# Forty-four drains at the head of TensorE's instructions in a fused scan and two-MLP kernel, and a constant of the same name

## The chip, the cores and the metric

One core of one Trainium2 chip runs the whole program. The metric is the device time of one execution in microseconds (us); lower is better. Engines are named as in the profile: PE is TensorE's products, PEld its weight loads, DVE is VectorE, ACT ScalarE, POOL GpSimd, SP SyncE; a name with a q (PEldq) is an engine's sequencer, which carries out drains and waits on semaphores.

## The reference

Three stages follow each other: a gated linear recurrence over 768 steps for 4 batches of 8 heads of width 48, an MLP with x·cos(x) between its products, and an MLP with a maximum over three products.

```python
for t in range(768):
    state = alpha[:, :, t, :, None] * state + einsum('bhd,bhe->bhde', k[:, :, t], v[:, :, t])
    y[:, :, t] = einsum('bhd,bhde->bhe', q[:, :, t], state)
x = y.transpose(0, 2, 1, 3).reshape(3072, 384)
h = x @ w_in                      # 384 -> 2048
x = (h * cos(h)) @ w_out          # 2048 -> 384
h = maximum(maximum(x @ w1, x @ w2), x @ w3)   # 384 -> 768
out = h @ w_out2                  # 768 -> 384
```

## The kernel before, in words

Tokens are worked on in six units of 512. The recurrence is turned into products on chunks of 64 steps: a **visit** (`visit`, lines 658 to 769) makes the scores, the state's increments and the outputs for one pair of heads, in small products of 48 or 64 rows that run on quarters of the array (lines 679, 683, 697 and 704). A visit that serves a new pair and an old one has 128 products in the trace, and each product has a weight load of its own, so it is 256 instructions. The first unit is done ahead in another form (lines 500 to 600).

The first MLP (`moe1`) takes 16 steps per unit, 96 in all. A step has nine products into a bank of PSUM (lines 780 to 782) and nine that add to three accumulators (lines 811 to 813), all of 128 rows and 512 columns; each number is split into a high and a low part in fp32r, so that three products stand for one. Visits are strewn between these steps until about 370 us. The second MLP works in 18 cells by a scheme with fewer products (lines 1164 to 1166), and `down` closes each third (lines 1073 to 1075). All of these are 128x512 products too.

What stands where is set by a planner in the program (`Program.order`): each operation has a duration, a due time and a number of instructions, and the planner lays them out in time on every engine, with PSUM banks. It counts TensorE's instructions in blocks of 256 (`BLOCK`, line 287) and tells by it where a large visit may stand; the warm-up operation counts as 28 instructions there. Where several PSUM banks are free, which of two tiles gets which bank follows from the order of a set of names, so that two builds of one text can differ in bank numbers, and in the number of waiting instructions on TensorE (80 to 85).

TensorE's first operation is `warm` (lines 1271 to 1274): seven products of the identity matrix with itself into banks that nothing reads. It waits for the identity, which POOL writes (masks.py, lines 197 and 199). After it come two products that clear accumulators (line 525), then the first transposes (line 562) and scores (line 502) of the first unit.

SBUF is allotted from two ends. From the left come the constants and the recurrence's tiles; at the right end stand the first MLP's weights `wih`, `wil`, `woh`, `wol`, the tiles `gg` with x·cos(x), `yy0`, and, last, a filler tile:

```python
PAD = 88                                                   # line 65
wp.tile([P, PAD], F32, name="pad")                         # line 335
np_.tile([P, PAD], F32, name="pad2")                       # line 842
```

The second MLP's tiles `bs_1`, `fs`, `wf` and `x` take the same right end later, with a filler of the same width behind them.

Of the kernel before, what the change touches and what calls it, by code (L numbers as in the profile page):

```python
# [64 lines left out]
PAD = 88  # L65
# [17 lines left out]
LOD = (1, 3)  # L83

W1E = 21
MOE_EARLY = 5
EARLY = 3
FIRST = -4
# [16 lines left out]
class Program:  # L105
# [16 lines left out]
    def op(self, eng, dur, fn, reads=(), writes=(), due=0.0, nbytes=None, port=False, tiled=False, count=6, tag=None):  # L122
        n = len(self.ops)
        if tag:
            self.tags[tag] = n
        deps = set()
        for k in reads:
            if k in self.last_write:
                deps.add(self.last_write[k])
        for k in writes:  # L130
            if k in self.last_write:
                deps.add(self.last_write[k])
            deps.update(self.readers.get(k, ()))
        for k in writes:
            self.last_write[k] = n
            self.readers[k] = []
        for k in reads:
            self.readers.setdefault(k, []).append(n)
        for k in {*reads, *writes}:
            if isinstance(k, tuple) and k[0] == "ps":  # L140
                self.of_bank.setdefault(k, []).append(n)
        deps.discard(n)
        port = port or (eng == "Pool" and nbytes is None)
        self.ops.append((eng, dur, nbytes, fn, sorted(deps), due, port, tiled, count))
        return n
# [116 lines left out]
def act(n, psum=False):  # L262
    return (0.05 if psum else 0.095) + 0.00084 * n
# [41 lines left out]
def tile_kernel(ctx, tc, aa, qk, vv, vr, wt, outT):  # L305
    nc = tc.nc
    ve, se, ge, pe = nc.vector, nc.scalar, nc.gpsimd, nc.tensor
# [464 lines left out]
    def moe1(i):  # L772
# [13 lines left out]
        qk = ("q", qn)  # L786
        m = i - MOE_EARLY
        op("Act", act(HB, True), lambda: se.activation(q.bitcast(I32), ps, AF.Copy, bias=0.25, scale=INV2PI), [hk], [qk], m)  # L788
# [438 lines left out]
    def build():  # L1227
# [41 lines left out]
        op("Pool", 1.0, setup_rest, (), ["tri"], due=-98)  # L1269

        def warm():
            for x, n in ((acc[0], P), (acc[1], D), *((x, D) for x in ps_b)):
                m = ident[:, 0:n].rearrange("p (a b) -> p a b", a=1).to_broadcast([P, 4, n])
                pe.matmul(x[:, 0:4 * n].rearrange("p (a b) -> p a b", a=4), ident, m, start=True, stop=True)

        op("PE", WARM, warm, ["ident"], [("acc", 0), ("acc", 1)], due=-99, count=28)

        events = []

        def at(t, f, *a):  # L1280
            events.append((t, len(events), f, a))
# [12 lines left out]
        for f in range(NF1):  # L1294
            at(W0 + f / 100, weight1, f, "i", f - W1E)
            at(W0 + f / 100, weight1, f, "o", f - W1E + 1)
        for i in range(NS):
# [159 lines left out]
```

## Time and profile before

| | |
|---|---|
| time, median of 3 runs | 738.92 us (738.33 to 741.87) |
| the profiled execution | 738.8 us, of which 737.0 us lie from its first instruction to its last |
| PE busy | 730.9 us (99%), 5813 products |
| PEld busy | 601.8 us (82%), 5813 loads |
| DVE busy | 541.2 us (73%) |
| ACT busy | 419.9 us (57%) |
| POOL busy | 305.3 us (41%) |
| DMA | 120.41 MB, mean 163 GB/s |

The profiled execution lies 0.1 us under the median of the runs; 1.8 us of it are outside the span. An end of a product is modelled in the profile, so a small wait can hide inside a busy time; starts are measured, and the distance between two starts is what can be read best. A reader looks first at the shares, then at TensorE's waits, then at the first 8 us in order of time.

### The profile page before, as it was taken

The page shows a single profiled execution, that of the slowest core. Times are in us where ns is not written, and L with a number is a line of the kernel's source. Part 1 is how long each engine was busy: PE and PEld are TensorE (multiplying, and loading weights), DVE is VectorE, ACT ScalarE, POOL GpSimd, SP SyncE. Part 2 cuts the span into 40 slices and gives each one's busy share as a digit, 9 for nine tenths or more (in the row PEclk, how much of TensorE's full clock was granted, in tenths as well). Part 3 has the DMA queues.
Part 4 walks back from the last instruction along what each step waited for, and adds up shares of the span by engine and source line. Part 5 has one row for each costly group of instructions (what it writes and reads, how often), then busy time and mean ns, then how long its engine had stood idle before and what let it go on. Part 6 is the DMA issues. An engine that isn't in the chain of part 4 may idle for free.

```text
span 737.0 us, 14864 instructions
## 1 busy us (share of the span) xinstructions
PE 730.9 (99%) x5813; PEld 601.8 (82%) x5813; DVE 541.2 (73%) x859; ACT 419.9 (57%) x801; POOL 305.3 (41%) x287
## 2 busy tenths in 40 slices
PE   9999999999999999999999999999999999999997
PEld 7787888888888888888888888888888888888886
DVE  8999996878887776865655666467787768677763
ACT  4878766666756666667644655443563345634233
POOL 6444433556533635454320211043465543614442
PEclk9999999999999999999999999999999999999999
DMA  9876544564644654554250111397636556246302
GB/s 320 297 225 219 165 126 134 178 221 160 196 146 154 189 179 139 182 178 150 96 207 0 44 43 44 135 370 291 215 104 197 202 176 204 79 149 204 132 1 85
DMA packets 47525, 120.41 MB, mean 163 GB/s; under 512 B 4736, under 2 KB 19968, under 8 KB 42464
## 3 DMA queue, kind: packets, MB, share of 16 engines
q1 hardware_dynamic: 47456, 119.48, 48.5%
q8 instruction: 45, 0.74, 0.4%
q14 instruction: 24, 0.20, 0.1%
HBM read 91.54 MB, written 25.95 MB: 159 GB/s over the span
## 4 chain that ended last, share of the span: by engine, by line
PE 92%; DVE 3%; DMA 2%; ACT 1%; issue 1%; POOL 0%; DVEq 0%; ACTq 0%; POOLq 0%
PE acc L811 9%; PE acc L813 8%; PE acc L812 8%; PE ps L780 8%; PE ps L781 8%; PE ps L782 8%; PE ps L1164 6%; PE ps L1166 5%; PE ps L1165 5%; PE acc L1164 3%; PE acc L1166 3%; PE acc L1165 3%; PE acc L1075 2%; PE acc L1073 2%; PE acc L1074 2%; DMA raw<-in_wt 2%
## 5 line engine op out<-in xcount | busy, mean ns | idle before, releaser
L780 PE MATMUL ps<-xt,wih 128*128 128x512 f32 x288 | 114.5, 398 | 0.0
L811 PE MATMUL acc<-gg,woh 128*128 128x512 f32 x288 | 114.4, 397 | 0.0
L813 PE MATMUL acc<-gg,woh 128*128 128x512 f32 x288 | 112.4, 390 | 0.0
L812 PE MATMUL acc<-gg,wol 128*128 128x512 f32 x288 | 112.2, 390 | 0.0
L782 PE MATMUL ps<-xt,wil 128*128 128x512 f32 x288 | 112.2, 390 | 0.0
L781 PE MATMUL ps<-xt,wih 128*128 128x512 f32 x288 | 112.1, 389 | 0.0
L789 DVE SCALAR_TENSOR_TENSOR q<-q,ps 128x512 f32<-128x512 int32 x96 | 65.5, 683 | 37.7 <-ACT q L788 37.2
L790 ACT ACTIVATE q<-q 128x512 f32<-128x512 f32 x96 | 60.4, 631 | 40.0 <-DVE q L789 39.7
L794 DVE TENSOR_TENSOR gg<-q,gg 128x512 fp32r<-128x512 f32 x81 | 63.5, 788 | 23.2 <-ACT gg L793 22.6
L792 DVE TENSOR_TENSOR q<-q,ps 128x512 f32<-128x512 f32 x81 | 55.2, 682 | 32.9 <-ACT q L790 32.3
L788 ACT ACTIVATE q<-ps 128x512 int32<-128x512 f32 x96 | 56.8, 593 | 38.8 <-PE ps L782 37.1
L793 ACT ACTIVATE gg<-q 128x512 fp32r<-128x512 f32 x81 | 51.1, 631 | 36.0 <-DVE q L792 31.6
L954 POOL TENSOR_TENSOR ar<-ar,ar 128x512 f32<-128x512 f32 x21 | 28.8, 1377 | 92.2 <-DVE as L963 67.6
L813 PEld LDWEIGHTS acc<-gg,woh 128*128 128x128 f32 x288 | 54.1, 188 | 12.2 <-DVE gg L806 0.4
L811 PEld LDWEIGHTS acc<-gg,woh 128*128 128x128 f32 x288 | 54.1, 188 | 11.6
L782 PEld LDWEIGHTS ps<-xt,wil 128*128 128x128 f32 x288 | 54.1, 188 | 11.4
L780 PEld LDWEIGHTS ps<-xt,wih 128*128 128x128 f32 x288 | 54.1, 188 | 11.3 <-issue 0.2
L812 PEld LDWEIGHTS acc<-gg,wol 128*128 128x128 f32 x288 | 54.1, 188 | 10.5
L781 PEld LDWEIGHTS ps<-xt,wih 128*128 128x128 f32 x288 | 54.1, 188 | 10.3
L1172 ACT ACTIVATE q<-acc 128x512 f32<-128x512 f32 x36 | 21.5, 597 | 69.2 <-PE acc L1166 68.5
L1183 POOL TENSOR_TENSOR xf<-q 128x512 f32<-128x512 f32 x18 | 24.5, 1361 | 81.5 <-ACT q L1172 81.5
L1036 ACT ACTIVATE fs<-x 128x512 fp32r<-128x512 f32 x42 | 26.2, 630 | 44.8 <-DVE x L1187 30.0
(190 smaller groups left out, 1730.2 us busy)
## 6 DMA issues: line engine op xcount, KB each, us to landing
bs<-bfd SPq DMA_DIRECT2D x36, 1024.0 KB, 5.0
raw<-in_wt SPq DMA_DIRECT2D x56, 384.0 KB, 4.1
bfd<-bs SPq DMA_DIRECT2D x32, 384.0 KB, 3.0
kq<-in_qk SPq DMA_DIRECT2D x20, 512.0 KB, 4.6
al<-in_aa SPq DMA_DIRECT2D x23, 261.0 KB, 3.3
x1r<-yy SPq DMA_DIRECT2D x18, 256.0 KB, 2.1
ar<-x1r SPq DMA_DIRECT2D x18, 256.0 KB, 3.1
v<-in_vv SPq DMA_DIRECT2D x23, 192.0 KB, 4.9
```

The costliest lines, as they stand in the source:

```text
L780: pe.matmul(ps, wi["h"][:, f, cc], xt[:, cc, 0], start=(cc == 0), stop=False)
L781: pe.matmul(ps, wi["h"][:, f, cc], xt[:, cc, 1], start=False, stop=False)
L782: pe.matmul(ps, wi["l"][:, f, cc], xt[:, cc, 0], start=False, stop=(cc == NR - 1))
L789: op("DVE", dve(HB), lambda: ve.scalar_tensor_tensor(q, q.bitcast(I32), -TWOPI, ps, ALU.mult, ALU.add), [hk], [qk], m, tag=("rest", i))
L790: op("Act", act(HB), lambda: se.activation(q, q, AF.Sin, bias=0.5 * math.pi), (), [qk], m, tag=("sine", i))
L794: op("DVE", dve(HB), lambda: ve.tensor_tensor(gl, q, gh.bitcast(F32), ALU.subtract), [qk, ("gh", gn)], [("gl", gn)], m, port=True)
L811: pe.matmul(acc[c], oh, gh, start=(f == 0), stop=False)
L812: pe.matmul(acc[c], ol, gh, start=False, stop=False)
L813: pe.matmul(acc[c], oh, gl, start=False, stop=(f == NF1 - 1))
L1164: pe.matmul(bank, bt[:, i, 0], at[:, 0], start=start, stop=False, skip_group_check=skip)
L1165: pe.matmul(bank, bt[:, i, 0], at[:, 1], start=False, stop=False, skip_group_check=skip)
L1166: pe.matmul(bank, bt[:, i, 1], at[:, 0], start=False, stop=stop, skip_group_check=skip)
```

## The change

Forty-four drains are issued on TensorE ahead of the first warm-up product. A drain makes an engine wait until its earlier work is done; there is none before these. They carry no wait on a semaphore and write nothing. The planner's number for the warm-up (28) stays, so the order of all other instructions on every engine stays as it was; each of TensorE's later instructions stands 44 places further in the stream, give or take the few waiting instructions in which two builds differ.

```diff
@@ -83,6 +83,7 @@
 LOD = (1, 3)
 
 W1E = 21
+PAD = 44
 MOE_EARLY = 5
 EARLY = 3
 FIRST = -4
@@ -1269,6 +1270,8 @@
         op("Pool", 1.0, setup_rest, (), ["tri"], due=-98)
 
         def warm():
+            for _ in range(PAD):
+                pe.drain()
             for x, n in ((acc[0], P), (acc[1], D), *((x, D) for x in ps_b)):
                 m = ident[:, 0:n].rearrange("p (a b) -> p a b", a=1).to_broadcast([P, 4, n])
                 pe.matmul(x[:, 0:4 * n].rearrange("p (a b) -> p a b", a=4), ident, m, start=True, stop=True)
```

The new constant has the name of the one in line 65, and both are set before the kernel is built, so the later one holds everywhere: the two fillers at the right end of SBUF are 44 columns wide instead of 88. The tiles in front of them move up by 160 bytes in each partition. `wih` begins at byte 118560 instead of 118400, and `wil`, `woh`, `wol`, `gg`, `yy0`, `bs_1`, `fs`, `wf` and `x` move alike. Before, all of these began at a multiple of 128 bytes; now they begin 32 bytes behind one. Tiles on the left side stay.

## Rows read from the trace of the kernel before

**Rows 1.** The page: TensorE's busy time and busy tenths, granted clock, chain by engine.

```profile
PE 730.9 (99%) x5813; PEld 601.8 (82%) x5813; DVE 541.2 (73%) x859; ACT 419.9 (57%) x801; POOL 305.3 (41%) x287
...
PEclk9999999999999999999999999999999999999999
...
PE 92%; DVE 3%; DMA 2%; ACT 1%; issue 1%; POOL 0%; DVEq 0%; ACTq 0%; POOLq 0%
```

**Rows 2.** TensorE's waits, the whole span: us in total, times, longest us.

```profile
PE acc L1274 <- POOL ident masks.py:199: 1.4, 1, 1.4
PE ps L679 <- DVE wol L402: 0.8, 1, 0.8
```

**Rows 3.** Busy time by stretch: us, then each engine's busy us with its instructions.

```profile
core 0: us, PE busy (x) PEld busy (x) DVE busy (x) ACT busy (x) POOL busy (x), PEclk, DMA share, GB/s
...
22.00:60.00 38.00, 37.06 (x376) 29.23 (x373) 35.59 (x66) 31.80 (x68) 17.95 (x19) 1.00 0.72 228
60.00:380.00 320.00, 320.00 (x3640) 263.62 (x3639) 244.68 (x424) 212.52 (x430) 146.39 (x148) 1.00 0.52 168
380.00:737.00 357.00, 353.22 (x1556) 291.37 (x1554) 242.57 (x333) 163.64 (x282) 128.51 (x93) 1.00 0.41 142
```

**Rows 4.** TensorE in order of time, 0 to 8 us: start, us, what [idle before].

```profile
1.43 2.71 PE L1274 MATMUL acc<-ident 128*128 128x512 f32 x4 [1.43 <-POOL ident masks.py:199]
3.94 3.21 PE L1274 MATMUL ps<-ident 128*128 128x192 f32 x10
6.84 0.76 PE L525 MATMUL acc<-gg 128*128 128x512 f32 x2
7.44 0.60 PE L562 MATMUL ps<-ident,kq 128*128 128x128 f32 x4
```

**Rows 5.** Sequencers at the program's start, line 1442: duration in ns min/median/max, first and last start.

```profile
L1442 PEldq DRAIN  x1: 8/8/8, 0.3 to 0.3; - x1
...
L1442 POOLq DRAIN  x1: 189/189/189, 0.4 to 0.4; - x1
...
L1442 ACTq EVENT_SEMAPHORE  x1: 17/17/17, 0.7 to 0.7; - x1
...
L1442 PEldq EVENT_SEMAPHORE  x1: 51/51/51, 0.7 to 0.7; - x1
```

**Rows 6.** Sequencers at the program's end, line 1448, same columns.

```profile
L1448 SPq DRAIN  x3: 7/7/7, 736.3 to 736.6; - x3
```

**Rows 7.** The page, DMA queues: packets, MB, share of 16 engines.

```profile
q8 instruction: 45, 0.74, 0.4%
```

**Rows 8.** TensorE in order of time around the visit at 175 us.

```profile
175.40 0.69 PE L679 MATMUL ps<-kq 48*64 48x64 f32 x32
...
177.28 0.50 PE L811 MATMUL acc<-gg,woh 128*128 128x512 f32 x1
177.61 0.39 PE L812 MATMUL acc<-gg,wol 128*128 128x512 f32 x1
```

**Rows 9.** DMA queues, packets that start from 176.7 to 177.0 us.

```profile
q8 instruction: 1, 0.02, 26.8%
```

**Rows 10.** TensorE in order of time around the visit at 233 us.

```profile
232.49 0.39 PE L811 MATMUL acc<-gg,woh 128*128 128x512 f32 x1
232.71 0.39 PE L812 MATMUL acc<-gg,wol 128*128 128x512 f32 x1
...
233.26 0.69 PE L679 MATMUL ps<-kq 48*64 48x64 f32 x32
...
235.14 0.50 PE L811 MATMUL acc<-gg,woh 128*128 128x512 f32 x1
```

**Rows 11.** DMA queues, packets that start from 234.5 to 235.0 us.

```profile
q8 instruction: 1, 0.02, 16.2%
```

**Rows 12.** DMA issues from 233 to 237 us: KB each, median us to landing.

```profile
kq<-in_qk SPq DMA_DIRECT2D x1, 512.0 KB, 5.0
...
raw<-in_wt SPq DMA_DIRECT2D x1, 384.0 KB, 5.3
```

**Rows 13.** Line 395 on ScalarE, which reads three tiles at two offsets: ns min/median/max.

```profile
L395 ACT ACTIVATE top<-raw x32: 612/646/666, 14.3 to 87.6; 128x384 f16<-128x384 bf16 x32
```

**Rows 14.** The page: products of the first MLP, by line: busy us, mean ns.

```profile
L780 PE MATMUL ps<-xt,wih 128*128 128x512 f32 x288 | 114.5, 398 | 0.0
```

## The prediction

> **What bounds the kernel now.** [...] But a product's end is modelled, so a busy share of 99% could hide small waits. Therefore the second view is TensorE's waits [rows 2]. The reader is to see that the whole list has two lines: 1.4 us before the first product, for the identity, and 0.8 us once, at 34 us. The third view is busy time by stretch [rows 3]: no idle time from 60 to 380 us, where the visits stand, and 0.94 us of 38 from 22 to 60 us. So the time is TensorE's own work in a row. What is put in front of it moves the end; what takes away a wait further back can give very little, because there is hardly a wait to take away.
>
> The change speaks of fetched chunks. They are the instruction queue's packets [rows 7]: 45 of 0.74 MB together, 16.4 KB each. TensorE carries out 5813 products, 5813 loads [rows 1] and some 85 waits, 11,700 instructions; by 45 that is 260, so a chunk is about 256 instructions, and 44 is a sixth of one.
>
> **Part 1: the drains themselves.** TensorE's first product starts at 1.43 us, released by POOL's identity [rows 4]. Its sequencer is through with the opening wait (51 ns, which begins at 0.7 us) and a branch at about 0.85 us [rows 5]. So 1.43 − 0.85 = 0.58 us of the drains' time lies beside the wait for the identity and costs nothing. No row shows 44 drains in a row. Their price is bounded from below by the record of a drain on TensorE, 8 ns, and from above by the longest drain at the start, POOL's 189 ns [rows 5]. A record isn't the whole step, though: SyncE's three drains at the end take 7 ns each by their records, yet begin over 0.3 us [rows 6], some of it waiting. The nearest row by engine is TensorE's own semaphore instruction, 51 ns; I add the 8 ns of a drain's record for the step between two and take 60 ns. That is 44 × 0.060 = 2.64 us, from 0.85 to 3.49 us, and the first product is late by 3.49 − 1.43 = 2.1 us. With 8 ns it is 0.85 + 0.35 = 1.20, before 1.43, so nothing; with 189 ns it is 0.85 + 8.3 − 1.43 = 7.7 us.
>
> [...]
>
> What does the lateness become? The warm-up products do nothing but run from 1.43 to 6.84 us [rows 4]; the first useful one, the clearing in line 525, follows them without a gap, and so does everything to 22 us. So all of TensorE's work moves by 2.1 us. It can be won back only where TensorE waits for something that doesn't itself move: that is the 0.8 us at 34 us, for `wol` from VectorE [rows 2]. That tile comes from weights that are loaded by DMA, which don't wait for TensorE, but VectorE and ScalarE work on them between operations of the first MLP that do. I take 0.5 of the 0.8 us as won back, with 0 and 0.8 as bounds. Sum of this part: +2.1 − 0.5 = **+1.6 us**.
>
> **Part 2: the moved chunks.** The cover that could fail is this: while a chunk is worked off, the next one is fetched. A visit has 256 instructions and takes 1.88 us (175.40 to 177.28) [rows 8], so it can use up a chunk faster than any other stretch. At that place the trace shows a fetch that begins in the visit, between 176.7 and 177.0 us, and takes 0.268 × 16 × 0.3 = 1.29 us [rows 9], so it lands not before 178.0. The products go on at 177.28 and 177.61 without a gap [rows 8]. So what TensorE has in hand reaches further than the visit's end. The visit at 233 us takes the same 1.88 us (233.26 to 235.14) [rows 10]. I set the stall to **0** both before and after: there is none to remove, and a shift of a sixth of a chunk makes no visit worse than the one at 175 us has been. The bounds: a gain up to the 0.8 us of the only wait after the start; a loss as worked out in rival B.
>
> **Part 3: the moved tiles.** Weights and `gg` begin 32 bytes behind a multiple of 128. TensorE reads no fp32r tile at such an offset now, so no row has the price. The nearest is ScalarE's line 395 [rows 13], whose three `raw` tiles alternate between a multiple of 64 and 32 beyond it: 612, 646 and 666 ns as least, median and most, no two levels. I take **0**; the upper bound from that row, 666 against 646 or 3%, would be 0.03 × 0.22 us (232.49 to 232.71, from one start to the next [rows 10]) on the first MLP's 6 × 288 = 1728 products [rows 14], 11 us; the lower bound is the same with the other sign, since nothing excludes it. (The second MLP's products that use a moved tile would add to either.) Both are far, and count only with the chance of rival C.
>
> **The sum.** 738.8 us (the profiled execution, 0.1 under the median of the runs) + 1.6 + 0 + 0 = **740.4 us**, a fifth of a per cent more. A measurement of this kernel can tell about 0.5%, 3.7 us, from no change; so I forecast no change that can be told.
>
> **The rivals.**
>
> A: the drains are hidden. With at most 13 ns a step all of them fit into the 0.58 us, and the time is 738.8 us. For it: the records of 7 and 8 ns. Against it: a step has to be more than a record, and TensorE's semaphore instruction has 51.
>
> B: a chunk comes late. By a count of the records (an estimate: a boundary is put about 1 us ahead of the start of its fetch) the boundary that now lies some 44 instructions inside the visit at 233 us falls on its start after the shift. The fetch there begins 1.3 us after the start of the visit (between 234.5 and 235.0, against 233.26) and takes 0.162 × 16 × 0.5 = 1.30 us [rows 10, 11]. If TensorE held only the chunk that it is working on, it would run dry at the visit's end, 1.88 us after its start, while the chunk asked for at its start lands 1.0 + 1.3 = 2.3 us after it: a wait of 0.4 us. If the packet has to queue as long as the data transfers of that stretch, 5.0 to 5.3 us [rows 12], the wait is up to 3.4 us. That gives 740.8 to 743.8 us. Against it stands the visit at 175 us, where the same didn't happen. [...]
>
> C: the moved tiles cost. This decides from 1.2 ns for each of the 1728 products, 2.1 us, which with the 1.6 us of part 1 passes 0.5%. Its place would be the spacing of products of the first MLP, all alike now at a mean of 398 ns by the page's modelled ends [rows 14]. At 2 ns it is 743.9 us, at 3% 751.8. Against it: line 395, and that 32 bytes is the step in which tiles are allotted here at all.
>
> D, which ends on the other side: a drain is dear on TensorE. From 111 ns a step the drains end at 0.85 + 4.9 = 5.7 us, the first product is 4.3 us late, and 3.8 us remain after the 0.5: slower than can be taken for no change. At 125 ns it is 743.2 us, at 189 ns 746.0. For it: POOL's drain with 189 ns [rows 5], and TensorE's sequencer has 51 ns on record for an instruction for which ScalarE's has 17 [rows 5]. Against it: the 8 ns record of TensorE's own drain.
>
> E: faster. The most that there is to gain is the 0.8 us; only tiles that read faster at their new places could pass 0.5%, and no row speaks for it.
>
> **How the numbers follow.** The forecast (a step of 13 to 110 ns, no stall, no price of the tiles) has 0.60, A 0.13, B 0.07, C 0.06, D 0.12, E 0.02. Slower by over 0.5% are D, nearly all of C and a little of B: 0.20. Faster is 0.02. The rest, 0.78, is within 0.5%. The range takes in A with the spread of the runs below it, all of the forecast (738.8 to 742.6) and the near part of D and B: 738.4 to 743.8 us; outside stay most of C, the far part of D, and E.
>
> **What would show it.** The first product of the warm-up begins at about 3.5 us instead of 1.43, with 44 drains ahead of it some 60 ns apart; line 525 follows at about 8.9 us; the wait of line 679 for `wol` is shorter than 0.8 us or gone. All large visits still take 1.88 us, and the means of lines 780 to 813 stay within a nanosecond. It is wrong if a visit is longer than 1.88 us or TensorE's list of waits has a new line (B), if these means move (C), or if the drains' spacing is over 110 ns (D) or under 13 (A).

## The result and the profile after

The changed kernel takes **750.76 us** (median of 5 runs, 750.24 to 751.65) against 739.09 us (738.33 to 741.87, 5 runs) for the kernel before: a ratio of 1.0148, 95% interval 1.0123 to 1.0172. It is slower by 1.5%, 11.7 us by the medians. The forecast was no change that can be told, 740.4 us in a range of 738.4 to 743.8.

The page of the changed kernel, cut to what [rows 1] and [rows 7] showed of the kernel before:

```profile
PE 741.5 (99%) x5813; PEld 601.6 (80%) x5813; DVE 541.7 (72%) x859; ACT 421.6 (56%) x801; POOL 304.3 (41%) x287
...
PEclk9999999999999999999999999999999999999999
...
q8 instruction: 46, 0.75, 0.4%
```

TensorE carries out the same 5813 products at a granted clock of 1.00 in the mean, as before, but is busy for 741.5 us instead of 730.9. The other engines are busy as long as before, within 2 us. So the time came as TensorE's own work, not as a wait. The list of TensorE's waits (us in total, times, longest us) says the same; it still has two lines [rows 2]:

```profile
PE acc L1277 <- POOL pad L1266: 4.0, 1, 4.0
PE ps L680 <- DVE wol L403: 0.3, 1, 0.3
```

The 4.0 us are the drains: the releaser named in the line was done at 3.3 us, the identity itself at 1.4 us as before, and what TensorE still had to work off was its own queue. (Line numbers after the change are one higher from line 86 on, and three higher behind the drains in the warm-up.) The drains' rows, and TensorE in order of time from the start, beside [rows 4]:

```profile
L1274 PEldq DRAIN  x44: 8/8/8, 0.9 to 3.9; - x44
```

```profile
4.00 2.71 PE L1277 MATMUL acc<-ident 128*128 128x512 f32 x4 [4.00 <-POOL pad L1266]
6.50 2.83 PE L1277 MATMUL ps<-ident 128*128 128x192 f32 x10
9.04 0.76 PE L526 MATMUL acc<-gg 128*128 128x512 f32 x2
```

Each drain's record is 8 ns, but from one to the next it is 68 or 69 ns (0.890, 0.959, 1.027 us and so on), for 40 of the 43 steps; with three of 98 to 108 ns the mean is 70.8. (None of them has work ahead of it to wait for. How a drain with such work looks, the end of the kernel before shows: at line 1448 TensorE's drain begins at 730.00 us and its record lasts 3.38 us, to 733.39, where the last product starts at 732.95.) The first product starts at 4.00 us instead of 1.43. That is 2.57 us of the 12.6 by which the span grew (737.0 to 749.6). (The warm-up itself takes 5.0 us here instead of 5.4, so line 526 is only 2.2 us late.) The visit that lay at 233 us shows no stall, 1.88 us from the first score to the first product behind it, as before [rows 10]:

```profile
237.75 0.69 PE L680 MATMUL ps<-kq 48*64 48x64 f32 x32
...
239.63 0.50 PE L812 MATMUL acc<-gg,woh 128*128 128x512 f32 x1
```

The rest has to be looked for in the stretch without waits. Busy time by stretch, beside [rows 3]:

```profile
60.00:380.00 320.00, 320.00 (x3615) 259.10 (x3615) 241.20 (x420) 211.12 (x426) 141.29 (x146) 1.00 0.51 162
```

It is as full as before, 320 of 320 us, and holds 3615 products instead of 3640. The products themselves take longer. The costliest groups (busy us, mean ns of one), beside [rows 14]:

```profile
L781 PE MATMUL ps<-xt,wih 128*128 128x512 f32 x288 | 116.2, 404 | 0.0
L812 PE MATMUL acc<-gg,woh 128*128 128x512 f32 x288 | 115.1, 400 | 0.0
...
L1076 PE MATMUL acc<-fs,wf 128*128 128x512 f32 x72 | 28.1, 390 | 0.0
L1075 PE MATMUL acc<-fs,wf 128*128 128x512 f32 x72 | 28.0, 390 | 0.0
```

and in the kernel before, the same lines, one number lower:

```profile
L811 PE MATMUL acc<-gg,woh 128*128 128x512 f32 x288 | 114.4, 397 | 0.0
...
L1075 PE MATMUL acc<-fs,wf 128*128 128x512 f32 x72 | 28.0, 389 | 0.0
```

Line 781 has gone from 398 to 404 ns and line 812 from 397 to 400, while lines 1075 and 1076 have stayed within 1 ns of their 389. Ends are modelled, so the exact measure is the distance from one start to the next. All of these distances, summed by the tile that a product streams, make up the whole difference between the last products' starts (732.95 and 745.57 us):

| what is streamed | products | before, us | after, us | difference |
|---|---|---|---|---|
| nothing yet: the first product's start | | 1.43 | 4.00 | +2.57 |
| `xt` | 1134 | 261.54 | 267.85 | +6.31 |
| `gg` | 866 | 201.55 | 203.55 | +2.00 |
| `as` | 594 | 135.40 | 137.72 | +2.32 |
| `fs` | 296 | 67.09 | 67.19 | +0.10 |
| all others | 2922 | 65.93 | 65.25 | −0.68 |
| sum | | 732.95 | 745.57 | +12.62 |

So 10.7 us came from 2890 large products that do the same work on tiles at other places. Which of them are slow, one trace shows by itself. The second MLP's cells take their weights `bs` in turn from `bs_0`, at the left end of SBUF, which has not moved, and from `bs_1`, at the right end, which has. The streamed `as` stands at the left in both. Two cells of the changed kernel, in order of time; the first two rows lie in one with `bs_0`, the last two in the next, with `bs_1`; the rows of each pair are 14 products apart:

```profile
503.41 0.39 PE L1165 MATMUL ps<-as,bs 128*128 128x512 f32 x1
...
506.58 0.39 PE L1167 MATMUL acc<-as,bs 128*128 128x512 f32 x1
...
514.38 0.39 PE L1165 MATMUL ps<-as,bs 128*128 128x512 f32 x1
...
517.65 0.39 PE L1167 MATMUL acc<-as,bs 128*128 128x512 f32 x1
```

With `bs_0` it is 3.17 us / 14 = 226 ns from start to start, as before the change. With `bs_1` it is 3.27 / 14 = 234 ns. It isn't the streamed tile's place, then, which is the same, and not the moved tile alone either: `fs` and `wf` have both moved, and their products have not become slower.

### The profile page after: what moved, and what is told of

Its sections match the earlier page's. It is cut to its first block, busy times and chain, and to the rows that moved or that the text cites. A ratio compares the mean times of both kernels' runs of the same rounds, so it can differ in the third digit from the quotient of the medians.

```text
span 749.6 us, 14910 instructions
## 1 busy us (share of the span) xinstructions
PE 741.5 (99%) x5813; PEld 601.6 (80%) x5813; DVE 541.7 (72%) x859; ACT 421.6 (56%) x801; POOL 304.3 (41%) x287
## 4 chain that ended last, share of the span: by engine, by line
PE 97%; ACT 1%; issue 1%; DVE 1%; POOL 0%; DVEq 0%; POOLq 0%; ACTq 0%
PE acc L812 9%; PE ps L781 9%; PE acc L813 9%; PE acc L814 9%; PE ps L782 9%; PE ps L783 9%; PE ps L1165 5%; PE ps L1166 5%; PE ps L1167 5%; PE acc L1165 3%; PE acc L1166 3%; PE acc L1167 3%; PE acc L1076 2%; PE acc L1075 2%; PE acc L1074 2%; PE ps L680 2%
## 5 line engine op out<-in xcount | busy, mean ns | idle before, releaser
L781 PE MATMUL ps<-xt,wih 128*128 128x512 f32 x288 | 116.2, 404 | 0.0
L783 PE MATMUL ps<-xt,wil 128*128 128x512 f32 x288 | 114.3, 397 | 0.0
L782 PE MATMUL ps<-xt,wih 128*128 128x512 f32 x288 | 114.1, 396 | 0.0
L1173 ACT ACTIVATE q<-acc 128x512 f32<-128x512 f32 x36 | 21.5, 596 | 70.8 <-PE acc L1167 70.0
```

The lines of the kernel that those rows point to most:

```text
L781: pe.matmul(ps, wi["h"][:, f, cc], xt[:, cc, 0], start=(cc == 0), stop=False)
L782: pe.matmul(ps, wi["h"][:, f, cc], xt[:, cc, 1], start=False, stop=False)
L783: pe.matmul(ps, wi["l"][:, f, cc], xt[:, cc, 0], start=False, stop=(cc == NR - 1))
```

## The experiments

Three theories were open. **T1**: a product is slower when the weights that are loaded beside it begin at another place than the streamed tile, counted within some period. **T2**: a tile that isn't at a multiple of 128 bytes is slow by itself. **T3**: the places in the fetched chunks, which is what the change speaks of. All kernels are the one before with the edit shown; the median of the kernel before was 739.7 to 739.9 us in these comparisons.

**The drains alone**, with a constant of their own, so that no tile moves:

```diff
 W1E = 21
+DRAINS = 44
...
         def warm():
+            for _ in range(DRAINS):
+                pe.drain()
```

> The 44 drains alone, with the fillers at 88 columns, so that no tile moves. If the moved tiles cost (theories T1, relative offset of weights and moving operand, and T2, absolute offset off a multiple of 128 bytes): first product at 4.0 us, time 740.5 to 741.5 us, product spacing 227 ns everywhere. If the moved places in the fetched chunks cost (T3): about 750 us with the spacing of the changed kernel (230 to 236 ns).

Measured: 739.67 us, ratio 0.9998 (0.9988 to 1.0008), 0.8 us under what T1 and T2 expected. In order of time, its first product starts as late as that of the changed kernel:

```profile
4.01 2.71 PE L1277 MATMUL acc<-ident 128*128 128x512 f32 x4 [4.01 <-POOL pad L1266]
...
9.46 0.80 PE L526 MATMUL acc<-gg 128*128 128x512 f32 x2
```

The 0.8 us wait for `wol` is gone from its waits. Of the 2.6 us by which it starts late 1.7 us are left at 36 us and 1.4 us at the last product. Its large products are 227 ns apart everywhere. T3 falls: all later instructions stand 44 places further, and that costs nothing that can be told.

**The tiles alone**, without a drain:

```diff
-PAD = 88
+PAD = 44
```

> The fillers at 44 columns and no drain: the tiles at the right end move by 160 bytes, nothing else. T1 and T2: 748 to 749.5 us, spacing of products that read xt with a moved weight 234 ns, first product at 1.4 us. T3: 739 us.

Measured: 749.39 us, ratio 1.0127 (1.0111 to 1.0142), with line 780 at 404 ns. One constant is most of the loss, 9.5 of 11.7 us. The runs of the changed kernel lie another 1.4 us higher (medians from two comparisons), which is what its drains would then cost.

**Another distance**, 128 bytes, at which every tile is again at a multiple of 128:

```diff
-PAD = 88
+PAD = 56
```

> No drain, fillers of 56 columns: the same tiles move by 128 bytes instead of 160. If what counts is the offset within 128 bytes (T1 and T2 alike): 739 us, spacing 227 ns. If any move of these tiles costs, whatever its size: 748 us or more. T3: 739 us.

Measured: 747.31 us, ratio 1.0102 (1.008 to 1.0123). This expectation missed for T1 with a period of 128 bytes, and T2 falls with it, since no tile is off a multiple of 128 here. If there is a period, it is longer. (The time is also a little under the 748 us expected if any move costs.)

**Both ends by 32 bytes**: a filler at the left end as well, so that all tiles leave the multiples of 128 together.

```diff
-PAD = 88
+PAD = 80
...
+    const.tile([P, 8], F32, name="pad0")
     ident = const.tile([P, P], F32, name="ident")
```

> No drain; every tile of both ends moves by 32 bytes, so that all fp32r operands begin 32 bytes behind a multiple of 128, as the moved ones did, but with no offset between them. T1 (only the offset between the weights that are being loaded and the operand that is streamed counts): 739 us, spacing 227 ns. T2 (absolute offset counts): 750 us or more, since now xt and as are off as well. T3: 739 us.

Measured: 740.48 us, ratio 1.0008 (0.9996 to 1.0021), and the products back at 227 ns:

```profile
L781 PE MATMUL ps<-xt,wih 128*128 128x512 f32 x288 | 114.5, 397 | 0.0
```

All tiles are off a multiple of 128, and nothing is slow. What counts is the offset between the two tiles. (Its profile has something else that was not expected; it stands in the last section.)

**256 bytes, and 512 bytes the other way:**

```diff
-PAD = 88
+PAD = 24
```

> The tiles of the right end move up by 256 bytes (a filler of 24 columns in place of 88), no drains. Theory T1 (a product is slower when the weights that are loaded under it begin at another place than its moving operand, counted within some period) with a period of 256 bytes: all products start 227 ns apart and the time is that of before, 739 to 740. T1 with a period of 512 bytes: 256 bytes are the farthest apart that two tiles can be, so xt x wih and as x bs_1 start 231 to 236 ns apart and the time is 746 to 751. Rival T5 (only the bytes by which the tiles are moved count, more bytes cost more: 128 bytes gave +7.4 us, 160 gave +9.5): 160 to 256 goes on rising, about 755.

```diff
-PAD = 88
+PAD = 216
```

> The tiles of the right end move down by 512 bytes (a filler of 216 columns), no drains: the largest move of all, but the offset between the two groups of tiles is the same in 512 bytes. T1: 227 ns everywhere, 738 to 741, same. T5 (the distance of the move counts) and T2 (the tiles' places themselves count): slower, 745 or more.

Measured: 739.81 us, ratio 0.9999 (0.9981 to 1.0018), for 256 bytes up, and 738.18 us, ratio 0.998 (0.9966 to 0.9993), for 512 bytes down, with every pair of tiles at 227 ns in both. Line 780 in the second kernel's groups:

```profile
L780 PE MATMUL ps<-xt,wih 128*128 128x512 f32 x288 | 114.5, 398 | 0.0
```

The two longest moves of the whole right end cost nothing, and 128 bytes did cost: the period is 256 bytes. The 0.2% by which the second is faster is below what can be told here; its products start 227 ns apart like those before.

**The first MLP's weights alone**, then **`gg` alone**, so that one or the other no longer agrees with what is read beside it. The first puts a filler ahead of `gg` (line 330), which moves only `wih` to `wol`:

```diff
-    gg_b = [wp.tile([P, 2, HB], F32R, name=f"gg{i}") for i in range(NG)]
+    wp.tile([P, 88], F32, name="pad3"); gg_b = [wp.tile([P, 2, HB], F32R, name=f"gg{i}") for i in range(NG)]
```

> A filler of 88 columns ahead of gg moves only wih, wil, woh, wol, down by 352 bytes (160 bytes past a multiple of 512); gg, bs_1, fs, wf and all of the left end stay. T1: xt x wih goes to 234 ns as in the change (about +6 us), and now gg x woh too, since the two stand 160 bytes apart (about 745 pairs by 3.5 to 7 ns, +2.6 to +5.2 us); as x bs_0, as x bs_1 and fs x wf stay at 227: 747 to 751 in all. Rival (gg x woh was slow in the change only because a run of xt x wih came before it): gg x woh as in the change, 230, total about 747 (+8). Rival T2 (each moved tile costs by its own place): xt x wih alone slow, gg at 227: about 745.

The second moves `wih` to `wol` down by a whole 512 bytes and `gg` (with `yy0`) up by 160:

```diff
-    gg_b = [wp.tile([P, 2, HB], F32R, name=f"gg{i}") for i in range(NG)]
+    wp.tile([P, 168], F32, name="pad3"); gg_b = [wp.tile([P, 2, HB], F32R, name=f"gg{i}") for i in range(NG)]
...
-    wp.tile([P, PAD], F32, name="pad")
+    wp.tile([P, 48], F32, name="pad")
```

> A filler of 168 columns ahead of gg and one of 48 in place of 88 after it: gg and yy0 move up by 160 bytes, wih to wol down by 512 bytes; bs_1, fs and wf stay. T1: xt x wih stays at 227 ns, gg x woh (160 bytes apart) goes up by 3.5 to 7 ns on about 745 pairs, as x bs_0 and as x bs_1 stay: +2.6 to +5.2 us, 742 to 745. Rival (the gg products of the change were slow only as an after-effect of the xt products ahead of them): 739 to 740, 227 ns everywhere. Rival (gg's writers, VectorE and ScalarE, meet the reads of TensorE): no change to speak of, 739 to 740, or gg's evictions longer than 0.398 us.

Measured: 749.47 us, ratio 1.0122 (1.0091 to 1.0154), and 744.64 us, ratio 1.0052 (1.0032 to 1.0073). In the first, both lines of the first MLP are slow, and the second MLP's `as` products are not; the groups by line of that kernel:

```profile
L780 PE MATMUL ps<-xt,wih 128*128 128x512 f32 x288 | 116.3, 404 | 0.0
L811 PE MATMUL acc<-gg,woh 128*128 128x512 f32 x288 | 116.1, 403 | 0.0
```

In the second, `xt` and its weights agree again and `gg` alone is off. Two runs of products of that kernel that follow each other, in order of time; from the first to the second row it is 14 products, from the third to the fourth 8:

```profile
128.43 0.39 PE L780 MATMUL ps<-xt,wih 128*128 128x512 f32 x1
...
131.60 0.39 PE L782 MATMUL ps<-xt,wil 128*128 128x512 f32 x1
131.83 0.40 PE L811 MATMUL acc<-gg,woh 128*128 128x512 f32 x1
...
133.70 0.39 PE L813 MATMUL acc<-gg,woh 128*128 128x512 f32 x1
```

3.17 / 14 = 226 ns for `xt`, and 1.87 / 8 = 234 ns for `gg`. Both kernels do what T1 says, within its numbers. What remains is why `gg` cost 2.0 us in the change, where it agrees with its own weights. There it follows slow `xt` products: in a run of `gg` right behind them the second product starts 234 ns before the next, the third to eighth 229 to 233, and from the tenth on it is 227; in the kernel before all of these are 227. So a slow run is paid for a little beyond its end. The kernel before has such a tail too, behind the small products of a visit: in a run of `gg` right behind them the second to sixth start 229 to 231 ns before the next, and from the seventh on it is 227. What makes the tail was not tried.

**Smaller offsets, and 96 bytes**, which is as far from a multiple of 256 as 160 is, on the other side. The first of the three (the others have 72 and 64 in its place):

```diff
-PAD = 88
+PAD = 80
```

> The tiles of the right end move up by 32 bytes, no drains. By now the runs show that xt x wih is free at 0 and 256 bytes, costs at 128 (232.4 ns) and at 160 (234 ns). Theory T1a (the cost depends on how far apart the two places are within 256 bytes, in either direction): 32 bytes is a small step apart, cheaper than 128: 228 to 231 ns, 741 to 745. Theory T1b (any offset that is no multiple of 256 costs about alike): 232 to 235 ns, 746 to 751. Rival T1c (only the part of 64 bytes or more counts): 227 ns, 739 to 740.

> The tiles of the right end move up by 64 bytes, no drains. T1a: between the 32 and the 128 bytes, 229 to 232 ns, 742 to 747. T1b: 232 to 235 ns, 746 to 751. T1d (what counts is the place within 64 bytes, and 128 and 160 differ for another reason): 227 ns, 739 to 740; the 128 bytes, which are a multiple of 64 and cost, speak against it already.

> The tiles of the right end move up by 96 bytes, no drains; this is as far from a multiple of 256 as the 160 bytes of the change are, on the other side. T1a and T1b, if the direction does not matter: as with 160 bytes, 234 ns for xt x wih, 748 to 750. If the direction matters (weights that begin ahead of the operand within the period cost otherwise than weights that begin behind it): anything between 740 and 755, which the pairs in the trace would show.

Measured: 747.04 us for 32 bytes (ratio 1.0093, 1.0064 to 1.0123), 749.64 us for 64 (1.0127, 1.01 to 1.0154), 749.2 us for 96 (1.013, 1.0103 to 1.0157). T1b holds best: 32 bytes cost nearly as much as 160. All together, with the offset of the weights against the streamed tile (in bytes, within 256, counted from the kernel before; by the tiles' sizes `gg` begins 192 × 256 bytes behind `woh` there, so that 0 is true agreement) and, in ns, the mean distance from a product's start to the next one's start, over all products that stream the first tile named while the next product's weights come from the other (745 or so for `xt` and `gg`, 290 to 296 for `as`; pauses of over 290 ns left out). The medians come from several comparisons, in which the kernel before gave 738.9 to 739.9 us:

| kernel | `xt`, `wih`/`wil` | `gg`, `woh`/`wol` | `as`, `bs_1` | median, us |
|---|---|---|---|---|
| before | 0: 227.1 | 0: 227.2 | 0: 227.2 | 738.92 |
| the change | 160: 234.1 | 0: 230.2 | 160: 233.4 | 750.76 |
| tiles alone | 160: 234.1 | 0: 230.3 | 160: 233.4 | 749.39 |
| 32 bytes | 32: 233.4 | 0: 228.7 | 32: 233.3 | 747.04 |
| 64 bytes | 64: 233.4 | 0: 229.4 | 64: 233.6 | 749.64 |
| 96 bytes | 96: 233.7 | 0: 228.8 | 96: 234.3 | 749.2 |
| 128 bytes | 128: 232.4 | 0: 229.5 | 128: 232.9 | 747.31 |
| 256 bytes | 0: 227.0 | 0: 227.3 | 0: 227.1 | 739.81 |
| 512 down | 0: 227.1 | 0: 227.2 | 0: 227.1 | 738.18 |
| both ends by 32 | 0: 227.0 | 0: 227.2 | 0: 227.3 | 740.48 |
| weights alone | 160: 233.6 | 160: 233.6 | 0: 227.2 | 749.47 |
| `gg` alone | 0: 227.8 | 96: 233.6 | 0: 227.2 | 744.64 |

**Twice the drains**, tiles as before; the edit shown is against the run with the drains alone, the ratio against the kernel before:

```diff
-DRAINS = 44
+DRAINS = 88
```

> 88 drains on an engine's queue ahead of the first product in place of 44, tiles as before (a constant of its own). From the run with 44 drains: 68.4 ns each, the first product at 4.01 us, and 1.4 us of the 2.6 left at 36 us, the wait at 34 us shrunk from 0.78 to 0.34. With 88 the first product starts at 7.0 us. Theory (each further drain is on the path once the cover is gone): at most 0.4 us of the further 3.0 us is won back, the time is 742 to 743.5 and the span 740.5 to 741.5. Rival (the drains lie beside loads that the start waits for anyway): 739 to 740, as with 44.

(The expectation gives 1.4 us at 36 us and a wait of 0.34 us for the run with 44 drains. These are the changed kernel's; with the drains alone it was 1.7 us, and the list had no such wait.)

Measured: 742.4 us, ratio 1.0039 (1.0025 to 1.0054). The drains' rows, and TensorE in order of time:

```profile
L1274 PEldq DRAIN  x88: 7/8/8, 0.9 to 7.0; - x88
```

```profile
7.10 2.71 PE L1277 MATMUL acc<-ident 128*128 128x512 f32 x4 [7.10 <-POOL kq L482]
```

The first product follows the last drain, not POOL, which was done with line 482 at 6.2 us. The second 44 drains put it back by another 3.1 us and cost 2.7 us of time (742.4 against 739.67, medians from two comparisons) and 2.8 of span (741.3 against 738.5). So a drain that nothing covers is on the path with nearly its whole step.

## Why the prediction was wrong

**What bounds the kernel** held: TensorE's work in a row. It is the reason why 6 ns a product could not hide anywhere.

**Part 3 failed, the moved tiles**: "I take **0**". It measured 10.7 us in the changed kernel, and the tiles alone cost 1.27%. The step that failed is this term, put at nothing by the choice of the nearest row. ScalarE's line 395 reads one tile at a time, so it could not show an effect that lies between two tiles. The prediction looked at a tile's own place, 32 bytes behind a multiple of 128; what the runs show in its place is the offset between weights and streamed tile, within 256 bytes. The upper bound of that step, 3% on the first MLP's products, 11 us, was close to what came, by luck, since it was the spread of a ScalarE line: 234 against 227 ns is 3%, in full on the products that stream `xt` over `wih` and `wil`, in part on those that stream `gg`, and on the second MLP's with `bs_1`. Rival C named the mechanism's place, the spacing of these products, and its sign came, line 780's mean moving from 398 to 404 ns; the forecast gave it 6 chances in 100 and left most of it outside the range. The argument against, that 32 bytes is the step of allotment, says only that no place is forbidden.

That the two tiles can meet is read from rows: a weight load takes 188 ns by its record, before as after, and products start every 227 ns, so a load runs beside the streaming of another product most of the time. A row of the kernel before:

```profile
L780 PEld LDWEIGHTS ps<-xt,wih 128*128 128x128 f32 x288 | 54.1, 188 | 11.3 <-issue 0.2
```

Load and product of this line both use all 128 rows, and over the whole span the loads are busy for 82% and the products for 99% [rows 1].

That it is TensorE's reads of weights and of the streamed tile which meet is an argument from the offset that decides, and not shown. Whether the load beside a product or its own earlier load matters stays open too, since almost all products have both at one offset. The nine borders from a cell with `bs_0` to one with `bs_1` say a little: there the last product's own weights, and those of the products ahead of it, are from `bs_0`, and only the load beside it is from `bs_1`. In the changed kernel it starts 236 or 237 ns before the next (before the change 226 or 227), which speaks for the load beside it. With 32 and 128 bytes it is 232 to 235 ns as well, but with 64 and 96 bytes only 225 to 229.

**Part 1, the drains, +1.6 us**: the mechanism was right. The step was mis-sized, 70.8 ns in the mean where 60 were taken, and so the first product is late by 2.57 us instead of 2.1; the wait for `wol` fell from 0.79 to 0.33 us in the changed kernel, 0.46 won back of the 0.5 expected. What is left at the end is less clear. The changed kernel lies 1.4 us above the tiles alone, near the forecast; but the drains alone gave −0.2 us (an interval of −0.9 to +0.6, which holds neither the 1.6 nor the 1.4 us that their profile still shows at the last product), while the second 44 cost 2.7. Where the missing microsecond of the first 44 lies stays open. The step of 68 ns and more speaks against rival D (over 110) and against rival A's mechanism (under 13), though the drains alone gave a time that can't be told from A's.

**Part 2, the moved chunks, 0**: it held for the changed kernel. The visit for which rival B reckoned with a stall takes 1.88 us after the change, and TensorE's list of waits has no new line. That there is no stall to remove held only for the execution that was read: some executions without drains have one, as the last section shows. Rival B's condition, that TensorE holds only the chunk that it is working on, was an assumption, and no run shows it.

## What to carry to other kernels

Where a stream of large fp32r products bounds a kernel, weights and streamed operand should begin at the same byte within 256; products that broke this started 232 to 234 ns apart here instead of 227, up to 3% more, while in the changed kernel TensorE's list of waits (two lines), its clock (1.00) and its busy share (99%) looked the same. (Products of other types or shapes were not tried.) A change that moves tiles in SBUF, even a filler's width, is a change of the products' speed until the spacing of their starts has been compared, pair of tiles by pair of tiles. And a constant that is set twice in one file can carry nearly the whole effect of an edit that seems to be about something else.

## What the runs showed of the hardware that was not expected

The offset between two SBUF tiles sets the spacing of this kernel's 128x512 fp32r products: 227 ns when it is a multiple of 256 bytes (229 to 230 for `gg` right behind slow `xt` products), 232 to 234 ns at 32, 64, 96, 128 and 160 bytes, with no clear growth from 32 on. Offsets between 160 and 256 were not tried.

A drain's record says 8 ns, and the step from one drain to the next on TensorE is 68 or 69 ns in most cases: the record's duration is not what a drain costs in a row.

A chunk of instructions seems to come late after all, in some executions. In the kernel with both ends moved by 32 bytes TensorE stops within a visit; in order of time, and the share of 16 engines of the instruction queue's packet from 308.45 to 308.75 us:

```profile
308.09 0.47 PE L680 MATMUL ps<-kq 48*64 48x64 f32 x19
...
309.48 0.31 PE L705 MATMUL ps<-kq,d 48*48 48x64 f32 x3
311.13 0.26 PE L705 MATMUL ps<-kq,z 48*48 48x64 f32 x2 [1.34 <-issue]
```

```profile
q8 instruction: 1, 0.02, 28.3%
```

The first row shows the last 19 of the visit's 32 scores; the visit starts at 307.86 us. The fetch, the 27th of this queue, starts 0.7 us later (308.56 us) and takes 0.283 × 16 × 0.3 = 1.36 us; TensorE stands still for 1.3 us. In the kernel before, the same visit starts at 308.59 us, but the 27th fetch started at 304.73, and nothing waits. The same stop, 1.1 to 1.3 us at the same visit, stands in the profiles of 256 bytes up, of the weights alone and of 96 bytes: 4 of the 11 profiled executions without drains, counting the kernel before, which has none. In these four the 27th fetch starts 0.4 to 0.8 us after the visit's start, in the other seven 2.4 to 4.1 us ahead of it. In the three with drains it starts 10 to 11 us ahead, and none of them has a stop there or elsewhere. So the moved places do take this fetch out of the visit's way. It may be part of the microsecond that is missing from the cost of the drains (4/11 of 1.2 us is 0.4 us, an estimate), but the executions that were not profiled can't show it. A stop as in rival B occurs, then, with 1.1 to 1.3 us about a tenth of the size of the tiles' cost. That the fetch causes it is read from its place alone, since the row of the stop names only `issue`. By the pages an execution has 45 or 46 fetches, of which at most one made TensorE wait. Why this fetch starts later in some executions was not tried.
